# Polysketch attention and ELU block in one kernel: first query group divided at the end, keys loaded first, weight rounding spread over three engines, narrower kv products

## The chip, the cores and the metric

One Trainium2 chip, one core of it. The metric is the device time of one execution in microseconds (us), as the median of several; lower is better. In a profile, PE is TensorE's matmul side and PEld its weight loads, DVE is VectorE, ACT is ScalarE, POOL is GpSimd and SP is SyncE; a `q` behind an engine name marks a DMA issue from that engine's queue.

## The reference, cut to what matters

```python
def phi(x):                                   # B=4 batches, H=4 heads, S=1088, D=32, r=8
    a = np.einsum('rd,bhsd->bhsr', S1, x)
    b = np.einsum('rd,bhsd->bhsr', S2, x)
    return np.einsum('bhsi,bhsj->bhsij', a, b).reshape(*x.shape[:-1], r * r)
q_p, k_p = phi(q), phi(k)                     # 64 features
kv  = np.einsum('bhsf,bhsd->bhfd', k_p, v)
z   = np.sum(k_p, axis=2)
num = np.einsum('bhsf,bhfd->bhsd', q_p, kv)
den = np.einsum('bhsf,bhf->bhs', q_p, z)[..., None] + 1e-06
x   = (num / den)                             # then (B,H,S,D) -> (4352, 128)
h   = x @ w_in                                # w_in 128 x 2048
g   = np.where(h > 0.0, h, np.exp(np.minimum(h, 0.0)) - 1.0)
out = g @ w_out                               # w_out 2048 x 128
```

`S1`, `S2`, `w_in` and `w_out` reach the kernel as 64-bit floats. The kernel loads them as pairs of 32-bit words and rounds them to 32-bit floats itself with bit operations; this is the "rounding" that the text is about.

## The kernel before

The work is a startup, then 9 query groups of up to 512 tokens, and for each group 8 steps, one for each pair of weight blocks `W[0]` to `W[7]`. A step is `mm1` (x @ w_in), `elu` (two ScalarE activations, one VectorE step called `gg`) and, two steps later, `mm2` (g @ w_out). I write mm1(0,7) for the first matmuls of group 0 on `W[7]`. The first group can only run a step when that step's W block has been rounded. The names of the tiles that matter: `Sab` is the rounded S, spread over the heads, with which keys and queries are multiplied; `ab` are these products, `kp` and `qp` the 64 features made from them; `qpT` is `qp` transposed, `xg` the x of a group, `pw` a product for the denominator.

The rounding, seven VectorE instructions on a 128x512 block:

```python
lo, hi = raw[:, :, 0], raw[:, :, 1]
nc.vector.tensor_scalar(ex, hi, 0x7FF00000, None, op0=AND)                        # L108
nc.vector.tensor_scalar(ex, ex, float(896 << 20), 0.0, op0=SUB, op1=MAX)          # L109
nc.vector.tensor_scalar(sg, hi, 0x80000000, None, op0=AND)                        # L110
nc.vector.scalar_tensor_tensor(sg, ex, 3, sg, op0=SHL, op1=OR)                    # L111
nc.vector.tensor_scalar(fr, hi, 0x000FFFFF, 0x00100000, op0=AND, op1=OR)          # L112
nc.vector.scalar_tensor_tensor(mant, lo, 2.0 ** -32, fr, op0=MUL, op1=ADD)        # L113
nc.vector.scalar_tensor_tensor(dst, mant, 2.0 ** -20, sg.bitcast(F32), op0=MUL, op1=MUL)  # L114: W
```

The loads, the kv products (64 columns: 32 of v and 32 ones, so that z comes out beside kv) and the division before the product:

```python
round_s = load_rounded([(S1, 0, D), (S2, D, 2 * D)], ...)      # sync queue
load_v(nc.scalar, 0)                                           # two DMAs on ScalarE's queue
load_hd(nc.sync, "k", k, 0, 0, KT); load_hd(nc.sync, "k", k, 0, KT, NT)
load_hd(nc.sync, "q", q, 0, 0, 8)
# ... weights, later batches
def KA(b, gi):       # kv += kp^T [v | 1]
    # ...
    nc.tensor.matmul(kv[64 * hp:64 * hp + 64, g2, :], kp[...], _ap(vt[b][...], [[VN - off, 2], [1, D]]), ...)
def KD(b):           # z -> SW (weights that give the denominator), kv -> kvS
    ...
def q2(g):           # denominator, reciprocal on 128x16, numerator features
    nc.vector.tensor_mul(pw, ...); nc.vector.tensor_reduce(den, pw, ...)
    nc.vector.reciprocal(den, den); nc.vector.tensor_mul(an, ...); nc.vector.tensor_mul(qp, ...)
```

The start and the main loop:

```python
transp(kT, "k", 0, 0, KT); transp(kT, "k", 0, KT, NT)
KF(0, 0); KF(0, 1); KF(0, 2)              # key features: Sab product, ScalarE copy ab, VectorE product kp
transp(qT, "q", 0, 0, 8)
KA(0, 0); KA(0, 1); KA(0, 2); KD(0)
q1(0); round_w[0](); q2(0); round_w[1](); q4(0); q5(0)
# ...
for n in range(steps + NP):
    g, cp = divmod(n, NP)
    mm1(g, cp)                             # (guards cut)
    # extra work of later groups and batches is placed here
    elu(g, cp)
    if n + 2 in range(2, NP):
        round_w[n + 2]()                   # behind gg(n) in VectorE's order
    mm2(*divmod(n - 2, NP))
```

## Time and profile before

| | before |
|---|---|
| median of 3 runs | 327.96 us (327.46 to 327.98) |
| profiled span, mean granted TensorE clock | 325.9 us, 0.972 |
| starts of mm1(0,0), (0,2) to (0,7) | 26.58; 37.53, 43.69, 49.53, 56.80, 61.58, 67.46 us |
| from mm1(0,7) to the end | 258.4 us |

How to read the views: the page begins with busy time and share for each engine, then strips of 40 digits, one for each fortieth of the span (8.15 us before), in tenths of busy time. A timeline line has the start, the duration, engine, source line, operation, output<-input tiles, shape, the number of instructions merged (`x4`) and in brackets the idle time before it and what ended it. A wait line has total us, count, longest.

### The profile page before, as it was taken

The numbers are of one execution on the slowest core, as the hardware profiler recorded it, in microseconds if no ns is written. First come the engines' busy times: TensorE is split into PE (matmuls) and PEld (weight loads), VectorE is DVE, ScalarE is ACT, GpSimd is POOL, SyncE is SP. The second block draws the span as 40 slices with busy tenths as digits, with TensorE's granted clock in tenths as the row PEclk, the third lists the DMA queues.
The fourth block names the chain that finished last, engine by engine and source line by source line (L and its number), as shares of the span: only waits on it lengthen the run. The fifth ranks groups of instructions, "written<-read, shape, count | busy, mean of one in ns | idle before, by whom it ended". The sixth has DMA issues, their size and how long they took to land. (4 is left out here: it accounts for less than half of the span.)

```text
span 325.9 us, 3678 instructions
## 1 busy us (share of the span) xinstructions
PE 294.3 (90%) x1468; PEld 148.2 (45%) x1468; DVE 163.9 (50%) x234; ACT 170.8 (52%) x220; POOL 1.8 (1%) x16
## 2 busy tenths in 40 slices
PE   2739384999999999999999999999999999999994
PEld 2723132444454444544454454544544444444582
DVE  4592969993443264552623364645233533443331
ACT  2213252454666656546565566546565766566661
POOL 2000000000000000000000000000000000000000
PEclk9955899999999999999999999999999999999999
DMA  7998000132010001000100010000100100010010
GB/s 203 369 325 231 5 0 0 46 92 70 0 33 2 0 0 32 2 0 2 33 0 2 0 32 0 2 0 10 24 1 2 32 0 0 0 34 0 0 32 17
DMA packets 9184, 13.34 MB, mean 41 GB/s; under 512 B 912, under 2 KB 6544, under 8 KB 9168
## 3 DMA queue, kind: packets, MB, share of 16 engines
q1 hardware_dynamic: 8624, 12.56, 13.3%
q10 hardware_dynamic: 544, 0.56, 0.7%
q8 instruction: 11, 0.18, 0.2%
q14 instruction: 5, 0.04, 0.0%
HBM read 10.88 MB, written 2.23 MB: 40 GB/s over the span
## 5 line engine op out<-in xcount | busy, mean ns | idle before, releaser
L341 DVE SCALAR_TENSOR_TENSOR gg<-e,h 128x1024 f32<-128x1024 f32 (+1 forms) x72 | 83.4, 1159 | 129.3 <-ACT e L339 127.1
L330 PE MATMUL h<-xg,W 128*128 128x512 f32 (+1 forms) x288 | 132.5, 584 | 12.1 <-DVE W L114 11.4
L350 PE MATMUL o<-gg,W 128*128 128x512 f32 (+1 forms) x288 | 131.1, 578 | 0.8 <-DVE gg L341 0.3
L338 ACT ACTIVATE e<-h 128x1024 f32<-128x1024 f32 (+1 forms) x72 | 70.6, 980 | 48.4 <-PE h L330 43.2
L330 PEld LDWEIGHTS h<-xg,W 128*128 128x128 f32 x288 | 54.7, 194 | 75.8 <-issue 72.3
L350 PEld LDWEIGHTS o<-gg,W 128*128 128x128 f32 x288 | 51.9, 190 | 51.1 <-issue 47.1
L339 ACT ACTIVATE e<-e 128x1024 f32<-128x1024 f32 (+1 forms) x72 | 72.7, 1010 | 2.3
L301 ACT COPY qpT<-qtp 128x512 f32<-128x512 f32 (+1 forms) x18 | 9.3, 565 | 23.8 <-PE qtp L300 23.8
L271 ACT COPY abw<-abwp 128x384 f32<-128x384 f32 (+1 forms) x9 | 4.2, 461 | 22.1 <-PE abwp L266 22.1
L204 DVE TENSOR_TENSOR kp<-ab 128x1024 f32<-128x1024 f32 (+1 forms) x12 | 11.3, 954 | 8.5 <-ACT ab L200 8.5
L200 ACT COPY ab<-abp 128x256 f32<-128x256 f32 (+1 forms) x12 | 3.8, 317 | 21.9 <-PE abp L196 21.4
L300 PE MATMUL qtp<-ident,qp 128*128 128x128 f32 x68 | 9.8, 290 | 5.2 <-DVE qp L287 5.2
L300 PEld LDWEIGHTS qtp<-ident,qp 128*128 128x128 f32 x68 | 8.6, 150 | 9.6 <-issue 9.6
L219 PE MATMUL kv<-v,kp 128*64 128x64 f32 (+1 forms) x288 | 12.1, 240 | 0.8 <-issue 0.8
L219 PEld LDWEIGHTS kv<-v,kp 128*64 128x64 f32 (+1 forms) x288 | 10.9, 153 | 3.3 <-issue 3.3
L287 DVE TENSOR_TENSOR qp<-an,abw 128x1024 f32<-128x1024 f32 (+1 forms) x9 | 10.5, 1166 | 0.3
L315 PE MATMUL xps<-qpT,kvS 64*32 64x256 f32 (+2 forms) x216 | 10.6, 323 | 0.0
L196 PEld LDWEIGHTS abp<-Sab,kT 128*64 128x64 f32 x136 | 6.0, 158 | 9.1 <-issue 5.3
L235 ACT COPY kvS<-kv 64x64 f32<-64x64 f32 x16 | 3.3, 207 | 12.8 <-DVE zm L228 12.7
L320 ACT COPY xg<-xps 128x256 f32<-128x256 f32 (+1 forms) x9 | 3.2, 361 | 12.2 <-PE xps L315 12.2
L266 PEld LDWEIGHTS abwp<-SW,qT 128*64 128x64 f32 x136 | 6.1, 140 | 7.3 <-issue 7.3
L196 PE MATMUL abp<-Sab,kT 128*64 128x64 f32 x136 | 7.6, 252 | 1.8 <-DVE kT L182 1.8
(47 smaller groups left out, 101.5 us busy)
## 6 DMA issues: line engine op xcount, KB each, us to landing
raw<-in_moe_w_in_dram SPq DMA_DIRECT2D x8, 256.0 KB, 5.5
raw<-in_moe_w_out_dram SPq DMA_DIRECT2D x8, 256.0 KB, 6.2
out_dram<-osb SPq DMA_DIRECT2D x13, 128.0 KB, 2.4
hd_k<-in_k_dram SPq DMA_DIRECT2D x3, 544.0 KB, 11.8
hd_q<-in_q_dram SPq DMA_DIRECT2D x3, 544.0 KB, 7.2
v<-in_v_dram SPq DMA_DIRECT2D x3, 288.0 KB, 12.2
v<-in_v_dram SPq DMA_DIRECT2D x3, 256.0 KB, 10.3
v<-in_v_dram ACTq DMA_DIRECT2D x1, 288.0 KB, 4.0
```

What stands on the lines that cost most here:

```text
L196: nc.tensor.matmul(abp[64 * u:64 * u + 64, j * 64:j * 64 + 64], kT[b][:, u * KT + i, :], Sab[:].rearrange("p h y -> p (h y)"), skip_group_ ...
L204: nc.vector.tensor_mul(kp[:rows, :n], _ap(a_, list(a_.ap[1:]) + [[0, R]]), _ap(b_, list(b_.ap[1:3]) + [[0, R]] + [b_.ap[3]]))
L219: nc.tensor.matmul(kv[64 * hp:64 * hp + 64, g2, :], kp[:rows, j, h].rearrange("p i j -> p (i j)"), _ap(vt[b][:rows, off:off + D], [[VN - o ...
L287: nc.vector.tensor_mul(qp[g][:, :m], _ap(a_, list(a_.ap[1:]) + [[0, R]]), _ap(b_, [b_.ap[1], [0, R], b_.ap[2]]))
L300: nc.tensor.transpose(p[:, o:o + P], qp[g][:, r:r + 2].rearrange("p t i j -> p (t i j)"), ident[:])
L301: nc.scalar.copy(qpT[g][:, 2 * hh:2 * hh + 2, :nh, :], p[:, :2 * nh * P].rearrange("p (h m s) -> p h m s", h=2, m=nh))
L315: nc.tensor.matmul(xp[w][D * h:D * h + D, :nh * P].rearrange("p (m s) -> p m s", s=P)[:, m0:m0 + m, s], kvS[64 * w:64 * w + 64, b, h, :], ...
L330: nc.tensor.matmul(h[:, c, :n], W[:, cp, c * P:c * P + P], xg[g][:, :n])
L338: nc.scalar.activation(e[:, :, :n], h[:, :, :n], RELU, scale=-1.0)
L339: nc.scalar.activation(e[:, :, :n], e[:, :, :n], EXP, scale=-1.0)
L341: nc.vector.scalar_tensor_tensor(gg[:, :, :n], e[:, :, :n], -1.0, h[:, :, :n], op0=ADD, op1=MAX)
L350: nc.tensor.matmul(ops[g][:, :n], W[:, cp, (2 + c) * P:(3 + c) * P], gg[:, c, :n], start=(cp == 0 and c == 0), stop=(cp == NP - 1 and c == 1))
```

## The change

The intent: get the first main matmul started sooner, and take VectorE's load off in the first 67 us, where TensorE waited for `W <- DVE`.

1. The keys load first on the sync queue; S goes to ScalarE's queue, ahead of v. S is rounded on 16 rows.
2. The first query group doesn't wait for z: numerator and denominator are both made as 32-column products, and the division is two reciprocals on 128x256 at the end.
3. Rounding: VectorE keeps four steps, ScalarE does the exponent (a relu with scale 8 and a bias), and for blocks 1 to 7 GpSimd does the last two multiplications. `W[1]` is rounded after the first group's x.
4. kv of batches 1 to 3 is made with 33 moving columns instead of 64, from a copy of v in a new layout that GpSimd makes (`V1`).

Smaller edits come with these: six buffers for the raw weights instead of eight, `ab` with three buffers, the first group's kv copied out by VectorE and ScalarE in turn.

```diff
-    def load_rounded(pieces, n, dst, bufs):
+    ebias = const.tile([P, 1], F32, name="ebias")
+    nc.vector.memset(ebias[:], -float(896 << 23))
+    def rounded(rows, n, dst, bufs, pool=False):
+            nc.vector.tensor_scalar(ex[:], hi, 0x7FF00000, None, op0=AND)
+            nc.scalar.activation(sg[:], ex[:], RELU, scale=8.0, bias=ebias[:rows])
+            nc.vector.tensor_scalar(fr, hi, 0x000FFFFF, 0x00100000, op0=AND, op1=OR)
+            nc.vector.scalar_tensor_tensor(mant[:], lo, 2.0 ** -32, fr, op0=MUL, op1=ADD)
+            nc.vector.scalar_tensor_tensor(sg[:], hi, 0x80000000, sg[:], op0=AND, op1=OR)
+            if pool:
+                nc.gpsimd.tensor_scalar(mant[:], mant[:], 2.0 ** -20, None, op0=MUL)
+                nc.gpsimd.tensor_mul(dst, mant[:], sg[:].bitcast(F32))
+            else:
+                nc.vector.scalar_tensor_tensor(dst, mant[:], 2.0 ** -20, sg[:].bitcast(F32), op0=MUL, op1=MUL)
 ... (loads)
+    load_hd(nc.sync, "k", k, 0, 0, KT)
+    raw_s, round_s = rounded(2 * R, D, S16[:], 1)          # its two DMAs on nc.scalar
     load_v(nc.scalar, 0)
-    load_hd(nc.sync, "k", k, 0, 0, KT)
     load_hd(nc.sync, "k", k, 0, KT, NT)
 ... (weights)
-                                   4 * P, W[:, cp, :], NP)
+                                   4 * P, W[:, cp, :], 6, nc.sync, cp > 0)
 ... (kv)
+    def V1(b):
+            nc.gpsimd.tensor_copy(v1[b][r]..., vt[b][r, :]...)         # once for each half
+        n = 2 * D if b == 0 else D + 1
-                                     _ap(vt[b][:rows, off:off + D], [[VN - off, 2], [1, D]]),
+                                     _ap(vt[b][...], [[VN - off, 2], [1, D]]) if b == 0 else v1[b][:rows, h * KT + i, :],
 ... (first group)
+    def q5_first():
+        # 32 products into p: numerators in [:256], denominators in [256:]
+        for w in range(2):
+            nc.scalar.activation(dn[:, w], p[:, w, 256:], COPY, bias=1e-6)
+        for w in range(2):
+            nc.vector.reciprocal(dn[:, w], dn[:, w])
+            nc.vector.tensor_mul(xg[0][:, 256 * w:256 * w + 256], p[:, w, :256], dn[:, w])
 ... (start)
+    q1_first()
+    q2_first()
     KA(0, 0)
     KA(0, 1)
     KA(0, 2)
-    KD(0)
-    q1(0)
+    KS(0)
+    q4(0)
     round_w[0]()
-    q2(0)
+    q5_first()
+    make_SX()
+    KZ(0)
     round_w[1]()
-    q4(0)
-    q5(0)
```

## The prediction

> **What bounds the kernel now.** I read the page's first two parts to see which engine is the bound, and when.
>
> ```profile
> PE 294.3 (90%) x1468; PEld 148.2 (45%) x1468; DVE 163.9 (50%) x234; ACT 170.8 (52%) x220; POOL 1.8 (1%) x16
> PE   2739384999999999999999999999999999999994
> DVE  4592969993443264552623364645233533443331
> PEclk9955899999999999999999999999999999999999
> ```
>
> From slice 9 on (one slice is 8.15 us) TensorE is full to the end, so its work after about 67 us is a block that the change hardly touches. What can be won lies in the first 67 us, where TensorE is two to eight tenths busy, VectorE is full, and the granted clock falls to half in slices 3 and 4. The waits of the first 70 us say what the main matmuls lack, and the timeline shows one period of it.
>
> ```profile
> PE h L330 <- DVE W L114: 11.4, 5, 5.1
> ```
>
> ```profile
> 33.65 0.42 DVE L108 TENSOR_SCALAR ex<-raw 128x512 uint32<-128x512 uint32 x1
> 34.10 0.43 DVE L109 TENSOR_SCALAR ex<-ex 128x512 uint32<-128x512 uint32 x1
> 34.45 0.42 DVE L110 TENSOR_SCALAR sg<-raw 128x512 uint32<-128x512 uint32 x1
> 34.90 0.69 DVE L111 SCALAR_TENSOR_TENSOR sg<-ex,sg 128x512 uint32<-128x512 uint32 x1
> 35.51 0.42 DVE L112 TENSOR_SCALAR fr<-raw 128x512 uint32<-128x512 uint32 x1
> 35.97 0.69 DVE L113 SCALAR_TENSOR_TENSOR mant<-raw,fr 128x512 f32<-128x512 uint32 x1
> 36.69 0.69 DVE L114 SCALAR_TENSOR_TENSOR W<-mant,sg 128x512 f32<-128x512 f32 x1
> 37.30 1.21 DVE L341 SCALAR_TENSOR_TENSOR gg<-e,h 128x1024 f32<-128x1024 f32 x1
> 37.53 3.40 PE L330 MATMUL h<-xg,W 128*128 128x512 f32 x4 [5.05 <-DVE W L114]
> ```
>
> Rounding one pair of weight blocks takes VectorE from 33.65 to 37.38, that is 3.7 us, and with the elu step (gg, 1.2 us) a period is 4.9 us where TensorE needs 4 x 0.43 for each of two groups, 3.44 us. The six later W blocks are ready at 37.4, 42.2, 49.4, 56.7, 61.4 and 67.4 us; the last one opens the full stretch. Ahead of it stands the start: key features, kv, z, query features, the first xg.
>
> ```profile
> 7.54 0.71 DVE L182 STREAM_TRANSPOSE kT<-hd_k 128x512 f32<-128x512 f32 x1 [0.60 <-DMA hd_k<-in_k_dram]
> 8.30 2.06 PE L196 MATMUL abp<-Sab,kT 128*64 128x64 f32 x32 [0.84 <-DVE kT L182]
> 11.19 3.72 PE L219 MATMUL kv<-v,kp 128*64 128x64 f32 x72 [0.83 <-issue]
> 22.17 1.94 PE L300 MATMUL qtp<-ident,qp 128*128 128x128 f32 x8 [5.25 <-DVE qp L287]
> 24.04 1.85 PE L315 MATMUL xps<-qpT,kvS 64*32 64x256 f32 x16
> 26.58 5.89 PE L330 MATMUL h<-xg,W 128*128 128x512 f32 x8 [0.69 <-DVE xg L321]
> ```
>
> The last digit group to read is in brackets: what was waited for. The keys waited for their transfer; the query transposes waited 5.25 us because VectorE did z, a whole rounding (15.8 to 19.5) and the five query steps first. The first main matmul starts at 26.58.
>
> **What the Trainium skill says.** "TensorE: Matmul & The Clock Gate", Part 1: the array runs at half clock until a window of about 3.4 us has been busy, and falls back after an idle one. The trace agrees: a main matmul is 0.85 us apart from the next in 26.6 to 31, 0.43 from 42 on, and the clock turned at about 17.4, 31.0, 37.9 and 41.3, multiples of 3.4 apart. The same part gives a least start-to-start of about 25 ns. "SBUF — State Buffer", section Who interferes with whom: a GpSimd instruction that reads SBUF and a VectorE instruction with two SBUF inputs, or in a two-port mode, exclude each other for a whole instruction. No overlap in this trace shows it. "GPSIMD Engine Reference", 3.1: a two-input fp32 operation of 2048 elements takes 4497 ns, so for 512 I estimate 1.1 to 1.2 us; this trace has only small copies (128x64: 0.24 us). "ScalarE: Activation LUTs", What ACT_TABLE_LOAD costs: 280 + 0.833 N ns with a pointer bias, hence about 0.7 us for 512; without one the trace has 0.63 us at 128x512.
>
> **The change part by part.**
>
> *Keys first, S on the other queue.* The key transfers are issued at about 0.7 and 1.4 us, not 1.5 and 2.2, and ahead of v. S is rounded on 16 rows with five VectorE steps, and Sab waits for one small matmul, not for three: I put Sab at 4.8 (was 6.25), the second key half at 5.3 to 6 (was 7.5), and the key features on TensorE at about 6.4, against 8.30. Gain 1.9 us.
>
> *First group without z.* Removed from the path: zm, wps, SW, and the steps pw, den, reciprocal, an (0.28 + 0.30 + 0.25 + 0.29, about 1.3 with gaps); the first rounding too is no longer ahead of qp. Added: q1_first stands ahead of kv on TensorE and needs the transposed queries, which follow the three kp products. So: features 6.4 to 8.5, kp to 10.7, transposes to 11.3, q1_first to 12.4, then kv for 3.7 us, to 16.1 (was 14.9). qp is done at 14.2, in the shadow of kv. Query transposes then run at 16.1 (was 22.2), 6 us earlier. q5_first has twice the matmuls (32 for 16): at half clock 1.85 becomes about 3.2 us, at full clock 1.2 becomes 2.0. It ends at 19.5 to 20.7; I take 20.2. W[0] is rounded beside it (VectorE 16.7 to 19.8).
>
> Now the division. The trace gives the reciprocal at two sizes:
>
> ```profile
> L281 DVE RECIPROCAL den<-den 128x16 f32<-128x16 f32 x8 | 2.0, 253 | 0.3
> L281 DVE RECIPROCAL den<-den 128x8 f32<-128x8 f32 x1 | 0.2, 206 | 0.0
> ```
>
> Eight more elements cost 47 ns, 5.9 ns each (a product costs 1.03: 219 ns at 64, 285 at 128). At 256 elements that is 206 + 248 x 5.9 = 1.67 us, twice: 3.3 us. With two products of 0.42 and the first ScalarE copy of 0.4, the path from q5_first to xg is 20.2 + 0.4 + 2 x (1.67 + 0.42) = 24.8. Behind it on VectorE and TensorE comes the deferred z product, 0.4, so the first main matmul is at 25.2: gain 1.4 of the 1.9 + 4 that the reordering seemed to give. TensorE has idled nearly 5 us by then and starts at half clock, as before.
>
> *W[1]* is now rounded after xg, not before: VectorE 25.6 to 27.7, GpSimd to about 29.6 (was 25.7). The first main step at half clock takes until 28.6, so W[1] opens a hole of about 1 us, which later waits absorb.
>
> *Rounding on three engines.* VectorE keeps two tensor_scalar and two two-input steps: 0.35 + 0.46 + 0.61 + 0.69 = 2.1 us (a tensor_scalar starts the next independent step after 0.35 and a dependent one after 0.46, a two-input step an independent one after 0.61: the starts in the rounding shown above), where it had 3.7. ScalarE gets 0.7, GpSimd about 0.65 + 1.2. The block is ready 2.1 + 1.9 = 4.0 us after its start, 0.3 later than now. VectorE's period falls to 3.3 us; but two other loops remain. ScalarE's order is relu(n), exp(n), rounding step (n+2), relu(n+1), and the rounding step waits for VectorE's ex, which waits for gg(n): 1.03 + 1.06 + 1.2 + 0.42 + 0.7 + hops = 4.6 us per step. And gg(n+2) waits for W[n+2], begun after gg(n): 2.1 + 1.9 + 1.9 (matmul, full clock) + 2.1 + 1.2 + hops of 0.4 = 9.6 for two, 4.8. So the period goes from 4.9 to 4.8: the 1.6 us that leave VectorE buy little here. They buy more where VectorE has other work: the query steps of group 1 (2.4 us) and the key transposes (1.3).
>
> Carried through (gg ends, before and after): gg(0) 33.7, 32.4; gg(1) 38.5, 36.9; gg(2) 45.7, 45.0; gg(3) 53.0, 50.8; gg(4) 57.8, 55.3; gg(5) 63.8, 61.8. W[7] at 61.8 + 4.0 = 65.8, or 66.3 if the kp product shuts GpSimd out for a while; before 67.4. Gain 1.1 to 1.6 us. This takes the third main step at half clock, since TensorE idles some 4 us before it; at full clock 1.7 us more are won, which I hold nearly even, so on average 2.2.
>
> *kv of 33 columns, batches 1 to 3.* 3 x 72 matmuls. This row has their weight loads, one per matmul:
>
> ```profile
> 69.83 1.02 PEld L219 LDWEIGHTS kv<-v,kp 128*64 128x64 f32 x32
> ```
>
> They start (1.02 - 0.14)/31 = 28.5 ns apart (0.14 is one load), the 96-column query products (0.69 - 0.14)/15 = 37. Were columns alone the bound, half of it would go, 3 us in all; with the 25 ns floor 3.5 x 216 = 0.75 us. The weight loads stay at 64 columns. I take 0.5. The copies into the new layout are GpSimd's, some 2 us per batch with 10 us to spare.
>
> Sum: 2.2 + 0.5 = 2.7 us, 325.2; a little more for effects of fewer VectorE steps that I can't place: 325.0.
>
> **The rivals.** (a) VectorE's sum is all that matters: seven roundings x 1.6 = 11 us less work, so up to 8 us gained, 319 to 321. For it speaks that VectorE is full in slices 4 to 8; against it that gg(0) and gg(2) already wait for ScalarE (5.4 and 2.35 us idle in the timeline). (b) GpSimd becomes the bound: its steps and VectorE's two-input steps exclude each other, 2.1 + 1.9 = 4.0 per block if all serial, still below 4.8; at twice my estimate it would be 6 us per block and the time 329 to 333. (c) The reciprocal eats the start: if q5_first stays cold and 1.67 is right, the start gains nearly nothing and the time is 326 to 328; if the reciprocal streams at about 1 ns per element, 2.5 us more are won, 322.5.
>
> **Range and chances.** The middle is 325.0. Rival (c) in its two forms and the clock at the third main step span 322 to 327.5; rival (a) reaches below. I take 321.2 to 327.9. Faster by over 2% means under 321.4, which needs (a), or the clock and the reciprocal both in favour: 0.17. Slower by over 2% needs over 334.5, beyond (b): 0.03. Within 2%: 0.80.
>
> **What would show it.** Right: key features near 6.4 us; two reciprocals of about 1.7 us; first main matmul near 25; TensorE still waiting for W[2] to W[7], now released by GpSimd, with ScalarE idle on ex; kv of later batches above 25 ns each; the last W near 65.5. Wrong: reciprocals near 0.4 us; W blocks under 4.2 us apart; GpSimd steps over 2.5 us a block; the full stretch starting before 62 or after 68; or kv near 15 ns.

## More of the kernel before

From mm1(0,7) on all weights are rounded and TensorE is full.

## The result, and the profile after

| | before | after |
|---|---|---|
| median | 327.97 us (327.46 to 328.17, 4 runs) | 331.05 us (330.78 to 331.42, 4 runs) |
| ratio after / before | | 1.0097 (95%: 1.008 to 1.0115) |
| profiled span, mean granted clock | 325.9 us, 0.972 | 329.7 us, 0.977 |
| start of mm1(0,0) | 26.58 us | 27.05 us |
| start of mm1(0,7) | 67.46 us | 71.48 us |

A ratio is the mean time of one kernel's fast runs over the mean time of the other's fast runs in the same rounds, so it isn't quite the ratio of the medians quoted. The change made the kernel slower by 1%, which is within 2% but above the range of the prediction (321.2 to 327.9). The granted clock is not the reason: its mean is slightly higher after. The 4.0 us by which mm1(0,7) is later account for the 3.8 us in the span.

First the page after: totals, then two of the strips.

```profile
PE 293.3 (89%) x1482; PEld 147.9 (45%) x1482; DVE 159.2 (48%) x210; ACT 176.0 (53%) x228; POOL 31.7 (10%) x37
...
PE   1655494599999999999999999999999999999994
...
POOL 2003425873000000000000000000000000000000
```

VectorE gave up only 4.7 us net (163.9 to 159.2), and GpSimd went from 1.8 to 31.7 us. Nearly all of that lies in slices 4 to 10, and of these 4, 5, 7 and 8 are the ones where TensorE isn't full. A 10% share of the span reads as an idle engine; the strip shows an engine at up to eight tenths in the place that counts. Who waits for whom, in the waits of the first 80 us after:

```profile
POOL mant L108 <- DVE mant L105: 38.6, 7, 21.2
...
ACT sg L103 <- DVE ex L102: 19.0, 7, 5.9
PE h L414 <- POOL W L109: 14.1, 5, 4.8
```

Before, TensorE waited 11.4 us for `DVE W L114`. Now it waits 14.1 us for `POOL W L109`. The wait was not removed; it changed its releaser and grew. The timeline after, one block from its first step to the matmul that it releases, as the counterpart of the rounding of before:

```profile
34.13 0.42 DVE L102 TENSOR_SCALAR ex<-raw 128x512 uint32<-128x512 uint32 x1
...
34.92 0.69 DVE L105 SCALAR_TENSOR_TENSOR mant<-raw,mant 128x512 f32<-128x512 uint32 x1
...
35.53 0.69 DVE L106 SCALAR_TENSOR_TENSOR sg<-raw,sg 128x512 uint32<-128x512 uint32 x1
35.70 1.86 POOL L108 TENSOR_SCALAR mant<-mant 128x512 f32<-128x512 f32 x1 [3.54 <-DVE mant L105]
...
37.64 1.27 POOL L109 TENSOR_TENSOR W<-mant,sg 128x512 f32<-128x512 f32 x1
38.47 0.73 DVE L102 TENSOR_SCALAR ex<-raw 128x512 uint32<-128x512 uint32 x1
38.97 3.78 PE L414 MATMUL h<-xg,W 128*128 128x512 f32 x4 [4.77 <-POOL W L109]
```

VectorE is done with the block at 36.2, 2.1 us after its start, as the prediction had it. But the block is ready at 37.64 + 1.27 = 38.91, 4.8 us after its start, where before took 3.7. The page's group lines show that this block is typical: mean 1853 ns and 1298 ns over the seven blocks.

```profile
L108 POOL TENSOR_SCALAR mant<-mant 128x512 f32<-128x512 f32 x7 | 13.0, 1853 | 38.6 <-DVE mant L105 38.6
...
L109 POOL TENSOR_TENSOR W<-mant,sg 128x512 f32<-128x512 f32 x7 | 9.1, 1298 | 0.6
```

The line at 38.47 shows the reverse side: the VectorE step `ex`, 0.42 us by itself, takes 0.73 while GpSimd's product runs. The query step of group 1 and the rounding beside the copies of v (`POOL L234`, 2.53 us at 59.57) are hit harder:

```profile
49.94 0.70 DVE L322 TENSOR_TENSOR pw<-abw 128x128 f32<-128x128 f32 x1
...
51.62 2.17 DVE L331 TENSOR_TENSOR qp<-an,abw 128x1024 f32<-128x1024 f32 x1
...
59.84 1.36 DVE L104 TENSOR_SCALAR mant<-raw 128x512 uint32<-128x512 uint32 x1
...
61.23 1.41 DVE L105 SCALAR_TENSOR_TENSOR mant<-raw,mant 128x512 f32<-128x512 uint32 x1
```

These took 0.28, 1.22, 0.42 and 0.69 us without GpSimd beside them. Now the start, again from the timeline after:

```profile
3.84 0.17 DVE L102 TENSOR_SCALAR ex<-raw 16x32 uint32<-16x32 uint32 x1 [2.03 <-DMA raw<-in_S_dram]
...
4.13 0.65 ACTq L84 DMA_DIRECT2D v<-in_v_dram  x1
...
4.83 0.32 ACT L103 ACTIVATE sg<-ex,ebias 16x32 uint32<-16x32 uint32 x1 [1.66 <-DVE mant L105]
...
6.58 0.23 DVE L189 TENSOR_TENSOR Sab<-sps,bmask 128x64 f32<-128x64 f32 x1 [0.76 <-PE sps L188]
...
9.70 2.69 DVE L225 TENSOR_TENSOR kp<-ab 128x1024 f32<-128x1024 f32 x3 [1.61 <-ACT ab L221]
...
21.96 1.74 DVE L371 RECIPROCAL dn<-dn 128x256 f32<-128x256 f32 x1
...
27.05 3.76 PE L414 MATMUL h<-xg,W 128*128 128x512 f32 x4
```

S is now the last thing to arrive. Its first rounding step starts at 3.84 (2.57 before), and the step that moved to ScalarE stands behind ScalarE's second issue of v (4.13 to 4.78) and starts only at 4.83. So Sab, which everything waits for, is later than before (6.58 against 6.03), although the keys are there early. The key products kp start at 9.70 against 9.86 before: 0.16 us gained of the 1.9 us predicted.

### The profile page after: what moved, and what is told of

It reads as the page before. It is cut to its first block, busy times and chain, and to the rows that moved or that the text cites. A ratio compares the mean times of both kernels' runs of the same rounds, so it can differ in the third digit from the quotient of the medians.

```text
span 329.7 us, 3711 instructions
## 1 busy us (share of the span) xinstructions
PE 293.3 (89%) x1482; PEld 147.9 (45%) x1482; DVE 159.2 (48%) x210; ACT 176.0 (53%) x228; POOL 31.7 (10%) x37
## 3 DMA queue, kind: packets, MB, share of 16 engines
q1 hardware_dynamic: 8592, 12.55, 13.2%
## 5 line engine op out<-in xcount | busy, mean ns | idle before, releaser
L414 PE MATMUL h<-xg,W 128*128 128x512 f32 (+1 forms) x288 | 132.8, 584 | 14.1 <-POOL W L109 14.1
L103 ACT ACTIVATE sg<-ex,ebias 128x512 uint32<-128x512 uint32 (+1 forms) x9 | 6.1, 679 | 20.6 <-DVE ex L102 19.0
L108 POOL TENSOR_SCALAR mant<-mant 128x512 f32<-128x512 f32 x7 | 13.0, 1853 | 38.6 <-DVE mant L105 38.6
L225 DVE TENSOR_TENSOR kp<-ab 128x1024 f32<-128x1024 f32 (+1 forms) x12 | 11.4, 966 | 9.3 <-ACT ab L221 9.3
L249 PEld LDWEIGHTS kv<-v,kp 128*64 128x64 f32 (+1 forms) x288 | 11.1, 156 | 2.3 <-issue 2.3
L249 PE MATMUL kv<-v,kp 128*64 128x33 f32 (+3 forms) x288 | 12.1, 242 | 0.0
L384 PEld LDWEIGHTS qtp<-ident,qp 128*128 128x128 f32 x68 | 7.9, 141 | 4.3 <-issue 4.2
L109 POOL TENSOR_TENSOR W<-mant,sg 128x512 f32<-128x512 f32 x7 | 9.1, 1298 | 0.6
L384 PE MATMUL qtp<-ident,qp 128*128 128x128 f32 x68 | 8.9, 273 | 0.0
```

The costliest lines, as they stand in the source:

```text
L108: nc.gpsimd.tensor_scalar(mant[:], mant[:], 2.0 ** -20, None, op0=MUL)
L109: nc.gpsimd.tensor_mul(dst, mant[:], sg[:].bitcast(F32))
L225: nc.vector.tensor_mul(kp[:rows, :n], _ap(a_, list(a_.ap[1:]) + [[0, R]]), _ap(b_, list(b_.ap[1:3]) + [[0, R]] + [b_.ap[3]]))
L249: nc.tensor.matmul(kv[64 * hp:64 * hp + 64, g2, :n], kp[:rows, j, h].rearrange("p i j -> p (i j)"), _ap(vt[b][:rows, off:off + D], [[VN - ...
L384: nc.tensor.transpose(p[:, o:o + P], qp[g][:, r:r + 2].rearrange("p t i j -> p (t i j)"), ident[:])
L414: nc.tensor.matmul(h[:, c, :n], W[:, cp, c * P:c * P + P], xg[g][:, :n])
```

## The experiments

**Theory A**, formed from the traces: the two rounding steps on GpSimd take 3.1 to 3.2 us per block and not the predicted 1.85, they delay VectorE besides, and this alone moves mm1(0,7) by about 5 us. **The rivals:** the loss lies in the start (the load order, or the new first group with its two reciprocals in series); it lies in the kv part, whose GpSimd copies stretch VectorE's steps; or VectorE's sum is what counts, so that taking work off GpSimd onto VectorE makes things worse. Each experiment edits the kernel after, unless it says otherwise. The expectations name theories and rivals by letters; A is the one above. Kernels that ran together share the runs of the kernel before, whose median differed between chips (328.2 to 328.9), so across groups I compare ratios and the marks in the traces. All 15 variants gave correct results.

### e1: the last rounding step on VectorE

```diff
-                                   4 * P, W[:, cp, :], 6, nc.sync, cp > 0)
+                                   4 * P, W[:, cp, :], 6, nc.sync, False)
```

> The changed kernel with the last rounding step of every W block back on VectorE (its five-step form, ScalarE's step kept); GpSimd does no rounding. Theory A (GpSimd's two steps, 3.1 us per block where 1.9 was estimated, delay each W block): W is ready 2.8 us after its ex step, not 4.8, the last W near 67 where it was 71.4, time 326 to 327.5. Theory B (the first group's division and the start lose the time): unchanged first xg, time stays at 330.5 to 331.5. Theory C (VectorE's sum is what matters): six blocks x 0.7 us more on VectorE, time 332 or more.

Measured: 327.19 us against 328.93, ratio 0.9944 (0.9898 to 0.999); span 324.1, mm1(0,7) at 66.00, 5.5 us sooner than in the kernel after. VectorE got 0.7 us more per block and the kernel became faster, so the rival of VectorE's sum is false. The other parts of the change are all still in this kernel, and it is a little faster than before. In the waits of its first 80 us the wait of TensorE for W is 8.5 us:

```profile
PE h L414 <- DVE W L111: 8.5, 3, 4.6
```

That is below the 11.4 of before. Theory A holds for the sign and the size.

### e2: kv with 64 columns again, no copies of v

```diff
-        n = 2 * D if b == 0 else D + 1
+        n = 2 * D
-        at(g, 4, V1, b)                      # and v1, its memsets and its use
```

> The changed kernel with the kv products of all batches at 64 columns, as before, and so without GpSimd's copies of v into a new layout. Theory A (GpSimd's rounding path): the copies at 59.6 to 62.1 delayed one W block, but the last W follows gg(5), which waited for other things: time 330 to 331. Theory D (the copies shut VectorE out, 0.9 + 0.7 us in the sixth rounding, and this reaches the end): 329 or less. On kv itself: if fewer columns saved anything, its products become longer here; the trace of the changed kernel says 28 ns apart as before, so no change.

Measured: 332.97 us (330.70 to 334.44), ratio 1.0115 (1.0052 to 1.0179); span 329.8, mm1(0,7) at 71.38. Against the kernel after (1.0097, 329.7, 71.48) this is nothing, in either direction. The 33-column product is worth 0, and its copies cost 0 as long as W's rounding is the bound: they do stretch VectorE's steps at 59.8, but mm1(0,7) comes no sooner without them. The timeline after shows it in the weight loads of batch 1's first 32 kv products:

```profile
73.83 1.02 PEld L249 LDWEIGHTS kv<-v,kp 128*64 128x64 f32 x32
```

The same 1.02 us for 32 as in the line that the prediction shows of before, and the matmuls beside them take 1.08 against 1.10 us. Halving the moving columns left the spacing at 28.4 ns. What sets that spacing, the weight load or a least time for each matmul, no run separates.

### e3: the first group as before (with z), all else as after

```diff
-    q1_first(); q2_first()
     KA(0, 0); KA(0, 1); KA(0, 2)
-    KS(0); q4(0); round_w[0](); q5_first(); make_SX(); KZ(0); round_w[1]()
+    make_SX(); KZ(0); KS(0); q1(0); round_w[0](); q2(0); round_w[1](); q4(0); q5(0)
```

> The changed kernel with the first query group done as in the kernel before (z, its weights, the five query steps, both roundings ahead of xg); the three-engine rounding stays. Theory A: the first main matmul starts about 25.6 (27.05 in the changed kernel, 26.58 before) because the first rounding has 0.8 us less on VectorE, W[1] is ready without a hole, but W[2] to W[7] still come from GpSimd: 329 to 330. Theory B (the first group is the whole loss): 327 or less.

Measured: 334.40 us (332.42 to 336.10), ratio 1.0163 (1.0096 to 1.0229); span 330.7, first main matmul at 28.09, mm1(0,7) at 72.50. I had expected an improvement and got a loss. In the trace the old first group is 1.0 us worse than the new one in this place; the times don't settle it, as the intervals overlap (two of the four runs took 332.4 to 332.7, two 336.1). Either way the two reciprocals of 1.74 us don't make the new form a loss. Part of the 1.0 us is not the first group's own: with q1_first gone, kv started at 12.05 and not at 11.19 as in the kernel before, most likely because the second half of v, issued at 4.08, landed 7.7 us later (the trace names `kp` as the releaser, whose first product was done at about 10.9).

### e4: the load order as before (S first on the sync queue, then keys)

```diff
+    # S: nc.sync.dma_start(raw_s[...]) ahead of the keys
-    load_hd(nc.sync, "k", k, 0, 0, KT)       # ahead of S
+    load_hd(nc.sync, "k", k, 0, 0, KT)       # behind S and v
```

> The changed kernel with S loaded first on the sync queue, then the keys, as before; all else as changed. The trace of the changed kernel has S landing at 3.8 us, where it was 2.5, and the first key features only 0.16 us earlier. If the new order is worth nothing, 330.5 to 331.5; if it costs (S now late, Sab late), up to 1 us less, 330; if the 1.9 us that I predicted for it are really there, 332.5 to 333.

Measured: 331.75 us, ratio 1.0079 (1.0037 to 1.0122); span 330.4, first main matmul at 27.70, mm1(0,7) at 72.11. In the trace the old order is 0.65 us worse; the times don't show it, as the interval holds the kernel after's ratio. It is small at most, and it isn't the loss. With e2 to e4, no other part of the change explains the 4 us.

### e5: the scaling by 2^-20 folded into ScalarE's bias

The factor 2^-20 can be put into the exponent: a bias of -(916 << 23) instead of -(896 << 23) for blocks 1 to 7. GpSimd keeps only the product. This takes the first of its two steps away without giving VectorE anything.

```diff
-                nc.gpsimd.tensor_scalar(mant[:], mant[:], 2.0 ** -20, None, op0=MUL)
+    ebias20 = ...; nc.vector.memset(ebias20[:], -float(916 << 23))     # bias if pool
```

> The changed kernel with the factor 2^-20 folded into ScalarE's bias for blocks 1 to 7, so that GpSimd keeps one step per block (the product, 1.27 us) and loses the 1.86 us tensor_scalar. Theory A (GpSimd's time per block is on the path of W): W ready about 3.45 us after its ex step where it is 4.8 now and 2.8 with VectorE alone; last W 67 to 68; ratio to the kernel before 0.985 to 0.997, near the run with rounding on VectorE. If VectorE's sum were the matter (theory C): no change, 1.009.

Measured: 328.84 us against 328.73, ratio 0.9995 (0.9943 to 1.0047); span 327.2, mm1(0,7) at 68.96, 2.5 us sooner than after. Less than I expected. Two things in its trace held it back: the main step at 56.14 ran at half clock (3.52 us for four matmuls instead of 1.9), and the last product took 2.19 us instead of 1.27, beside VectorE's two-input kp. The direction supports A; how much one step was worth by itself, this run doesn't tell, since the clock moved as well.

### e6: the last two VectorE rounding steps swapped

In the kernel after, GpSimd's scaling starts beside VectorE's two-input step on `sg` (35.70 beside 35.53 to 36.22). Swapped, it starts after both. If the long 1.86 us is its own, it stays; if it is being shut out, it shrinks.

```diff
+            nc.vector.scalar_tensor_tensor(sg[:], hi, 0x80000000, sg[:], op0=AND, op1=OR)
             nc.vector.scalar_tensor_tensor(mant[:], lo, 2.0 ** -32, fr, op0=MUL, op1=ADD)
-            nc.vector.scalar_tensor_tensor(sg[:], hi, 0x80000000, sg[:], op0=AND, op1=OR)
```

> The changed kernel with VectorE's last two rounding steps exchanged (sign and exponent first, mantissa last), so that GpSimd's tensor_scalar, which starts on the mantissa, no longer meets the two-input VectorE step; the next VectorE work beside it is elu, with one input in PSUM. If its 1.86 us is 1.36 of work and 0.5 of being shut out by that step: 1.3 to 1.4 us now. If 1.86 is the step's own cost: 1.8 to 1.9 still. The time hardly matters here: 330 to 332.

Measured: one run, 335.24 us, its state unknown; a time I don't use. In its trace (the page's group line):

```profile
L108 POOL TENSOR_SCALAR mant<-mant 128x512 f32<-128x512 f32 x7 | 10.4, 1490 | 43.6 <-DVE mant L106 43.6
```

1490 ns by itself, against 1853: so 0.37 us per block was waiting for VectorE, and 1.49 is the step's own cost. Neither of the two expected values came out exactly; the truth lies between, nearer to the lower. The swap itself is bad: it adds a wait for ScalarE in front of `mant`, and mm1(0,7) comes at 75.37.

### e7: S first, v issued behind S's rounding

Built to test the reading of the start: S back to the front of the sync queue, and v's two DMAs on ScalarE's queue only after ScalarE's part in rounding S.

```diff
-    load_v(nc.scalar, 0)
     round_s()
+    load_v(nc.scalar, 0)                     # and S, keys on nc.sync as in e4
```

> The changed kernel with S first on the sync queue, the keys behind it, and v issued from ScalarE only after ScalarE's step of the S rounding. In the changed kernel the keys landed at 4.1 and 4.9 us, but S at 3.8, and ScalarE's step for S started at 4.83, right behind its second v issue (4.13 to 4.78). If that held the start: Sab near 4.8 (6.58 in the changed kernel), key features near 6.3, first main matmul 26 (27.05), time about 1 us less, ratio 1.005 to 1.008. If the landing of v or keys then holds it instead: no gain, 1.009 or more.

Measured: 337.71 us (334.71 to 338.11, 6 runs), ratio 1.028 (1.024 to 1.032). Four of the six took 337.5 to 338.1; the profile is of one of the two faster ones: span 332.9, mm1(0,0) at 31.03, mm1(0,7) at 74.64. Sab came at 4.58, 2.0 us sooner than after, as expected. The rest was not expected. The timeline of this run:

```profile
5.54 4.02 ACTq L84 DMA_DIRECT2D v<-in_v_dram  x2
...
9.60 0.65 ACT L221 COPY ab<-abp 128x256 f32<-128x256 f32 x2 [6.46 <-DMA raw<-in_moe_w_out_dram]
...
17.39 4.30 PE L249 MATMUL kv<-v,kp 128*64 128x64 f32 x72 [2.81 <-DMA v<-in_v_dram]
```

ScalarE's two issues took from 5.54 to 9.56, and its first copy of key features, which stands behind them in its order, started at 9.60: an early Sab won nothing. Then v itself, queued behind the first weights, held kv up until 17.39 (14.03 after). So S early is possible, but not at v's cost; and an issue on a compute engine's queue is work in that engine's order.

### e8: fold (e5), and the rounding ahead of elu

The two loops that the prediction named come from program order: the rounding of block n+2 stands behind gg(n) on VectorE, and ScalarE's step waits for `ex`. Here the rounding is issued before elu(n).

```diff
             mm1(g, cp)
+        if n + 2 in range(2, NP):
+            round_w[n + 2]()
 ... elu(g, cp)
-        if n + 2 in range(2, NP):
-            round_w[n + 2]()
```

> As the run with the factor folded, and besides each rounding is issued ahead of the elu step of its turn, not behind it, so that VectorE and ScalarE round W[n+2] while they would wait for h of turn n. If the loops that I named (rounding behind gg(n), relu(n+1) behind the rounding) set the pace, blocks come 3.4 to 4 us apart, the last W before 60, ratio 0.965 to 0.98. If GpSimd's throughput or VectorE's sum sets it, no better than the folded run.

Measured: 323.15 us (322.05 to 323.90) against 328.73, ratio 0.9824 (0.9767 to 0.988); span 322.2, mm1(0,7) at 64.05, 7.4 us sooner than after and 4.9 sooner than e5; the ratio is just short of the expected 0.965 to 0.98. Part of the gain is the clock, which no run takes apart from the order: TensorE, with shorter waits, ran at full clock from 34 to 58 us here (1.95 us for mm1(0,2)), where after it was at half from 38 to 42 (3.78 us).

### e9: the rounding ahead of elu, GpSimd's two steps kept

```diff
             mm1(g, cp)
+        if n + 2 in range(2, NP):
+            round_w[n + 2]()                 # e8's edit, without e5's
 ... elu(g, cp)
-        if n + 2 in range(2, NP):
-            round_w[n + 2]()
```

> The changed kernel with the rounding issued ahead of elu, GpSimd's two steps (3.1 us) kept. If the place in the order is what costs, most of the gain of the previous run comes here too: ratio 0.975 to 0.99. If GpSimd's latency alone costs, with the loop it makes: near 1.005.

Measured: 327.10 us against 328.73, ratio 0.9945 (0.9884 to 1.0006), where 0.975 to 0.99 was expected; span 325.4, mm1(0,7) at 67.16, 4.3 us sooner than after. GpSimd's scaling still takes 1866 ns and its product 1297 in this trace. So the order of issue is worth 4.3 us even with the slow GpSimd, and e8, with the fold, is 3.1 better; but at mm1(0,6) the two are only 0.9 us apart (56.04 and 55.14). The wait of TensorE for W from GpSimd falls from 14.1 to 3.6 us. What remains late here is the stretch from mm1(0,6) at 56.04 to mm1(0,7): the copies of v stretch VectorE's steps there (in this trace `mant` 1.36 and 1.41 beside them, kp 1.93 instead of 1.23), and TensorE's clock was at half from 62 to 66 us, so that four matmuls of mm2 took 3.78 us. How the stretch divides between the two I can't say.

### e10: fold, early rounding, and `ex` one block further ahead

The rounding is split: `ex` of block n+3 is placed before gg(n), ScalarE's step for it after exp(n), the rest of block n+2 before elu(n). No engine then waits at the head of its queue for a step that stands behind the current elu.

```diff
             mm1(g, cp)
+        if n + 2 < NP:
+            round_w[n + 2].parts[2]()        # fr, mant, sg on VectorE, product on GpSimd
+        if n + 3 < NP:
+            round_w[n + 3].parts[0]()        # ex
 ... elu(g, cp)
+        if n + 3 < NP:
+            round_w[n + 3].parts[1]()        # ScalarE's step
-        if n + 2 in range(2, NP):
-            round_w[n + 2]()
```

> The folded factor and the early rounding, and besides VectorE's ex step of block n+3 is issued ahead of gg(n) and ScalarE's step behind exp(n), so that neither waits for the other. In the run before it the main matmuls of turns 2 to 5 came 4.4 to 5.9 us apart, waiting for gg, in a loop gg, ex, ScalarE's step, relu, exp. If this loop was the rest: 3.4 to 3.9 us apart, ratio 0.972 to 0.98. If something else holds it (the query steps of group 1, v's copies on GpSimd): as that run, 0.982.

Measured: 318.27 us (317.92 to 318.47) against 328.27, ratio 0.9683 (0.9652 to 0.9715); span 316.4, mm1(0,7) at 58.28, 13.2 us sooner than after. Its strip, and its largest wait for a releaser at the main matmul, from the waits of the first 80 us:

```profile
PE   1666888999999999999999999999999999999993
```

```profile
PE h L426 <- DVE gg L437: 2.5, 2, 1.4
```

In slices 5 to 7 TensorE is at eight tenths, where it had four, nine and four after. The matmuls' wait for W from GpSimd, 14.1 us after, is down to 0.2. Here too the clock is part of the gain: from 34 to 300 us it is full, and mm1(0,2) takes 1.96 us where it took 3.78 after:

```profile
34.40 1.96 PE L426 MATMUL h<-xg,W 128*128 128x512 f32 x4 [1.39 <-DVE gg L437]
```

### e11: e10 with 64 columns (e2) and e7's load order

```diff
 # e10, and
-        n = 2 * D if b == 0 else D + 1
+        n = 2 * D
-    load_v(nc.scalar, 0)                     # ahead of S's rounding
+    load_v(nc.scalar, 0)                     # behind it; S and keys on nc.sync
```

> The previous run with kv at 64 columns again (no copies of v on GpSimd) and S first, v behind (as in the first run of this set). GpSimd's copies shut VectorE out for 0.85 us in one rounding and 0.6 in one kp product; without them and with an earlier start: 1 to 2 us less than the previous run, ratio 0.967 to 0.977.

Measured: 321.79 us, ratio 0.9791 (0.9756 to 0.9825); span 320.2, mm1(0,0) at 31.87. A miss: with the late v its first main matmul comes 4.8 us later than e10's and its span is 3.8 us longer.

### e12: the kernel before with nothing but the three-engine rounding

```diff
 # before.py: the seven VectorE steps replaced by the kernel after's rounding
-                                   4 * P, W[:, cp, :], NP)
+                                   4 * P, W[:, cp, :], NP, cp > 0)
```

> The kernel before with the rounding on three engines alone (GpSimd's two steps for blocks 1 to 7), all else as before. Theory A (this part is the loss): slower than before by 4 to 5 us, ratio 1.012 to 1.017, with W[2] to W[7] late. Theory B (the loss is in the first group or the load order): 1.000 or below, as VectorE has 1.6 us less per block.

Measured: 331.05 us (329.90 to 331.79) against 328.27, ratio 1.007 (1.0032 to 1.0109); span 329.4, mm1(0,7) at 70.97. The ratio is smaller than I expected, the direction right. In the span it is 3.5 us slower than before, of the 3.8 us that the whole change lost; in the ratios 0.7% of 1.0%, with intervals that overlap. Of the 3.5 us, 0.9 is a later first main matmul (27.48 against 26.58): the second key half landed later, the first rounding waited 0.8 us for ScalarE's step, and kv ran slower. In this trace TensorE waits 11.1 us for W, released by GpSimd, in four waits:

```profile
PE h L336 <- POOL W L118: 11.1, 4, 5.6
```

Theory A is shown from both sides: the one part put in brings most or all of the loss, and GpSimd's steps taken out again remove it (e1).

### e13: S, keys, v, queries, weights, all on the sync queue

```diff
-    load_v(nc.scalar, 0)
     load_hd(nc.sync, "k", k, 0, KT, NT)
+    load_v(nc.sync, 0)
     load_hd(nc.sync, "q", q, 0, 0, 8)
```

> The changed kernel with all first loads on the sync queue in the order S, keys, v, queries, weights, so that ScalarE's queue has no issues. If S and ScalarE's blocked queue held the start: Sab near 4.6 (as in the run with v behind), key features near 6, ScalarE's first copy near 7.5 (9.29 in the changed kernel), kv not waiting for v, first main matmul 25 to 26 (27.05), ratio 1.003 to 1.007. If keys or queries now land too late, first main matmul 27 or later, 1.009 or more.

Measured: 330.13 us, ratio 1.0048 (0.9992 to 1.0104); span 329.2, mm1(0,0) at 26.30 (27.05 after), mm1(0,7) at 70.51. Sab came at 4.50 and kv had no wait for v. But the transpose of the second key half waited 1.75 us for its transfer, until 7.22, so most of the 2 us that Sab won was lost again; 0.75 us is left at the first main matmul.

### e14 and e15: the best parts together

e14 is e10 with e13's load order; e15 is e14 with 64 columns and without the copies of v.

```diff
 # e10, and for e14 and e15
-    load_v(nc.scalar, 0)
+    load_v(nc.sync, 0)                       # behind the keys; S first
 # for e15 also
-        n = 2 * D if b == 0 else D + 1
+        n = 2 * D
-        at(g, 4, V1, b)
```

> The best run so far (factor folded, rounding early, ex ahead of gg) with that load order. If gains at the start pass through to the end: 1 to 1.5 us less than that run, ratio 0.963 to 0.967; if they are absorbed by the waits for gg between 31 and 55 us: unchanged, 0.968.

> The previous run with kv of all batches at 64 columns and no copies of v on GpSimd. If the copies cost anything at the end, up to 0.7 us less than the previous run; if not, the same within 0.3; if 33 columns saved TensorE time, more.

Measured: e14 317.21 us (316.99 to 317.69), ratio 0.9654 (0.9591 to 0.9716), mm1(0,7) at 56.90. e15 316.23 us (315.57 to 316.85), ratio 0.9622 (0.9567 to 0.9677), span 315.0, mm1(0,7) at 56.21. e15 is the fastest kernel, and 3.8% faster than the kernel before. Its lead over e14 is 1 us in the medians and 0.5 in the spans; in the ratios the intervals overlap, so I call it not settled, and so is e14's over e10. The traces do show what the copies of v cost once W's rounding is no longer the bound: from mm1(0,6) to mm1(0,7) take 6.9 us in e10 and e14, and 5.4 in e11 and e15, which have no copies. In e15 a later first main matmul (26.50 against 25.71) gives 0.8 of these 1.5 us back.

### The marks of all runs

Starts in us in the profiled run; the ratio is against the kernel before on the same chip.

| run | mm1(0,0) | mm1(0,7) | span | median | before there | ratio |
|---|---|---|---|---|---|---|
| before | 26.58 | 67.46 | 325.9 | 327.97 | | |
| after | 27.05 | 71.48 | 329.7 | 331.05 | 327.97 | 1.0097 |
| e1 last step on VectorE | 26.50 | 66.00 | 324.1 | 327.19 | 328.93 | 0.9944 |
| e2 kv of 64 | 27.20 | 71.38 | 329.8 | 332.97 | 328.93 | 1.0115 |
| e3 old first group | 28.09 | 72.50 | 330.7 | 334.40 | 328.93 | 1.0163 |
| e4 old load order | 27.70 | 72.11 | 330.4 | 331.75 | 328.93 | 1.0079 |
| e5 fold | 27.37 | 68.96 | 327.2 | 328.84 | 328.73 | 0.9995 |
| e6 swap (state unknown) | 27.89 | 75.37 | 333.5 | 335.24 | 328.73 | none |
| e7 v behind S | 31.03 | 74.64 | 332.9 | 337.71 | 328.27 | 1.028 |
| e8 fold, early | 27.43 | 64.05 | 322.2 | 323.15 | 328.73 | 0.9824 |
| e9 early | 26.54 | 67.16 | 325.4 | 327.10 | 328.73 | 0.9945 |
| e10 fold, early, split | 27.09 | 58.28 | 316.4 | 318.27 | 328.27 | 0.9683 |
| e11 e10, e2, e7 | 31.87 | 61.57 | 320.2 | 321.79 | 328.27 | 0.9791 |
| e12 before, rounding only | 27.48 | 70.97 | 329.4 | 331.05 | 328.27 | 1.007 |
| e13 all on sync | 26.30 | 70.51 | 329.2 | 330.13 | 328.23 | 1.0048 |
| e14 e10, e13 | 25.71 | 56.90 | 315.5 | 317.21 | 328.23 | 0.9654 |
| e15 e14, e2 | 26.50 | 56.21 | 315.0 | 316.23 | 328.23 | 0.9622 |

## Why the prediction was right or wrong

The prediction said 325.0 (321.2 to 327.9); measured were 331.05. "Within 2%" held, the range and the sign did not; that it held is no merit of the mechanism. By its own steps:

**"GpSimd about 0.65 + 1.2" failed, and this is the main step.** The product was sized right (1.27 against 1.2), and so was ScalarE's step (0.72 against 0.7). The scaling took 1.86 and not 0.65. The 0.65 was the one number in that sum without a row behind it: the trace of before had no GpSimd step of that size, only small copies. e6 splits the miss: 1.49 is the step's own cost, and the other 0.37 is gone when VectorE's two-input step is out of its way, so I read it as waiting for that step. Some of the extra is hidden, since the scaling can start after `mant` and need not wait for `sg`; the block is ready 4.8 us after its start, predicted 4.0, before 3.7. e1 and e12 show that this part makes the loss (e12 most or all of it). Rival (b) of the prediction, GpSimd as the bound with 329 to 333 us, is the nearest to what happened, and the time falls into its range; but GpSimd was not full (busy for 23.1 of the 42 us from 28 to 70), it was late. It was held off by a sum of busy time, "4.0 per block if all serial, still below 4.8", where the latency of the chain counted: the W block is not ready until the last of its steps.

**The carried-through times.** The ends of gg, predicted and measured:

| | gg(0) | gg(1) | gg(2) | gg(3) | gg(4) | gg(5) | W[7] ready |
|---|---|---|---|---|---|---|---|
| predicted | 32.4 | 36.9 | 45.0 | 50.8 | 55.3 | 61.8 | 65.8 to 66.3 |
| after, measured | 34.2 | 38.6 | 48.0 | 54.9 | 59.3 | 66.5 | 71.4 |

The miss is 1.7 us at gg(1), which is the start; it grows to 4.1 at gg(3) and 4.7 at gg(5), and the last rounding (4.0 predicted, 5.0 measured) brings it to 5.1 or more. The largest growth, 2.4 us from gg(1) to gg(3), has three parts: the slow W, a VectorE that did pw in 0.70 (0.28) and qp in 2.17 (1.22) beside GpSimd, so 1.4 us of stretching, and gg(3) behind both. These overlap, and I don't split the 2.4 us any further. The third main step at half clock isn't part of this miss, as the table was made with it. But the sum of the prediction counted on half of the 1.7 us that full clock would bring, 0.85; the step took 3.78 us at 38.97, and this came to nothing.

**The exclusion of VectorE and GpSimd was named but not priced.** The prediction named the section on it and said that no overlap in the trace of before showed it. After it shows: 0.42 to 0.73 and to 1.36, 0.69 to 1.41, 1.22 to 2.17. It allowed 0.5 us in all, at W[7].

**"Keys first: gain 1.9 us" failed.** It came out as 0.16 us at kp. The keys landed in time (their transposes, at 6.72, waited for no transfer), but S, whose part was only guessed, came 1.3 us later than before, and the step given to ScalarE stood behind a DMA issue of ScalarE's own queue (4.13 to 4.78). Sab: predicted 4.8, measured 6.58. e7 and e13 bring Sab to 4.58 and 4.50, so the reading is right, but then v or the second key half is late, as if the first transfers competed, and of 2 us at Sab 0.75 at most reaches the first main matmul (e13).

**"First main matmul at 25.2" was 1.85 late**, at 27.05. The reciprocals were right (1.67 worked out from two sizes, 1.74 measured), and so was the idea that they eat most of what the order gains. The late key features carried through, and the first reciprocal started 0.5 us later than its input allowed (21.96; ScalarE's copy was done at about 21.5), since the last step of W[0]'s rounding, begun at 21.35, stood ahead of it on VectorE; the prediction had this rounding end at 19.8. Of rival (c) in its first form, the start gaining nearly nothing (-0.5 us) is what came true, but its time of 326 to 328 did not, since the loss lies elsewhere. In e3's trace the new first group is still better than the old one, by about 1 us, in this surrounding.

**"W[1] opens a hole of about 1 us":** 1.41 us of wait at mm1(0,1), since W[1] came at 32.16 and not at 29.6. This is the same step of 0.65, seen again, on top of the late start.

**"kv of 33 columns: 0.5" was 0.** The spacing stayed at 28.4 ns with 33 columns (e2; the prediction gave the same quotient as 28.5).

**"The 1.6 us that leave VectorE buy little here", because of two loops: right.** It is the best part of the prediction. e1 shows that VectorE's sum isn't the bound, and freeing the loops gives what the change hoped for: e9 4.3 us, e8 7.4, e10 13.2, full clock included. Rival (a), up to 8 us from VectorE's sum, is false for the change as it stands. But its hope was not absurd: the time was there, behind the order of issue and not behind the amount of work. What was said for it, "VectorE is full in slices 4 to 8", misread the strip: the digits there are 2, 9, 6, 9, 9 (and TensorE has nine tenths in slice 4, above the "two to eight").

What stays open: how the 2.4 us from gg(1) to gg(3) split; whether e15's lead over e14 is real; how much of e5's gain its half-clock step took, and how much of e8's and e10's gain is the clock. No run gives the kernel before the early order with its seven VectorE steps, so whether the 13 us need the rounding on three engines at all isn't known.

## What to carry to other kernels

Moving work to an idle engine helps only if the chain through it is no longer than the one that it replaces: add up the latency of the chain, from the first step to what it releases, and measure the new engine's step at the size in question before trusting a small number for it. When a wait such as "PE <- DVE W" is on the path, ask first what stands in front of that W in the program order of each engine; here a different order of the same steps, with one step folded away, was worth 13 us against the kernel after (9 against before), where taking 1.6 us per block off VectorE had lost 4. A compute engine's own DMA issues are part of its order (e7), and an earlier arrival of one of the first transfers can be a later arrival of another: with S early, v was late in e7 and the second key half in e13.

## What the Trainium skill lacked or had wrong

- "GPSIMD Engine Reference", 4.1 Engine selection, says of one-input operations that they are "roughly line-rate". Here a one-input `tensor_scalar` on 128x512 fp32, in place, took 1.49 us undisturbed (e6), longer than the two-input product on the same size (1.27 us) and 3.5 times the 0.42 of VectorE's `tensor_scalar` steps of that size. The 4497 ns for 2048 elements of section 3.1 did carry over to the product: a quarter is 1.12.
- "SBUF — State Buffer", Who interferes with whom, was right in kind: a VectorE `tensor_scalar` went from 0.42 to 0.73 and 1.36 us beside GpSimd's product and copies, and two-input steps from 0.69 to 1.41 and from 1.22 to 2.17. For the size it says, of VectorE's two-port modes, that the other engine is blocked for the whole instruction; for two SBUF inputs it gives none. Here the second lost most of what was left of the first: `qp` 0.95 of 1.1 us, `ex` 0.31 of 0.44, GpSimd's scaling 0.37 of 0.52. But `pw`, begun with 1.43 us of the scaling left (49.51 to 51.37), lost only 0.42 and ran beside the rest, as far as GpSimd's recorded spans, which are rough, show it.
- "TensorE: Matmul & The Clock Gate", LDWEIGHTS, gives the number of columns over 1.2, so 53 ns for 64 columns. The loads of 64 columns here start 28.4 ns apart at full clock ((1.02 - 0.14) / 31), and they stay there with 33 or 64 moving columns; that is nearer to the floor of about 25 ns in the same page. The kv products alternate between two column halves of the array; whether their loads overlap for that, no run shows.
- No page that I read gives VectorE's reciprocal a rate. Here 128x16 took 0.25 us and 128x256 took 1.74, so 6.2 ns per element ((1.74 - 0.25) / 240), six times a product.
- No page that I read says that DMA issues on ScalarE's queue hold up its compute. In e7 two issues took from 5.54 to 9.56 us, and the copy behind them started at 9.60.
